# 88 unused columns at the end of the right-hand arena of a fused attention and two-layer feed-forward kernel

## Chip, core and metric

One core of one Trainium2 chip. The metric is the device time of one execution in microseconds (us); three runs of the kernel before were timed and their median is taken. One more execution was profiled, and all rows below come from it.

## What is computed

The program takes `q`, `k`, `v` of shape (4, 8, 576, 64), a feature matrix `omega` (128, 64) and five weight matrices, and runs three layers on 2304 tokens of width 512:

```python
def phi(x):
    proj = np.einsum('bhsd,md->bhsm', x, omega)
    h = proj - np.sum(x * x, axis=-1, keepdims=True) / 2.0
    return np.exp(h - np.max(h, axis=-1, keepdims=True)) / np.sqrt(m)
q_p, k_p = phi(q * scale), phi(k * scale)
kv = np.einsum('bhsm,bhsd->bhmd', k_p, v);  z = np.sum(k_p, axis=2)
x = (q_p @ kv) / (q_p . z + 1e-06)              # attention, (2304, 512)
h = x @ w_in                                    # (2304, 2048)
x = (h * sigmoid(h)) @ w_out                    # first feed-forward layer
g = x @ w_gate;  val = x @ w_val                # (2304, 1536) each
x = (g * sigmoid(g) * val) @ w_out2             # second feed-forward layer
```

All of it is in float32, and the weights come in as float64.

## The kernel before

**Stages.** Attention runs first (lines 678 to 966, up to about 122 us of the span). Then come four matmul phases: up 1 (`x @ w_in`, `up_phase`, line 1060, about 122 to 301 us), down 1 (`@ w_out`, `down_phase`, line 1308, to about 488 us), up 2 (`w_gate` and `w_val`, to about 756 us) and down 2 (`@ w_out2`, to the end).

**One product.** Each big matrix product is cut in 2 x 2 blocks and done with seven block products (`PROD`, `ORDER`) in place of eight. Every float32 operand is split in a high and a low part of type float32r, and a product is three matmuls: high weights by high data, high by low, low by high. So both up phases run one loop (line 1090) and both down phases another (line 1465), over matmuls of one kind: 128 x 128 weights and 384 moving columns.

```python
for l, r in ((wh, xh), (wh, xl), (wl, xh)):     # products, L1090
    nc.tensor.matmul(ps[b][:, :N], cut(l, j * P, P), cut(r, j * N, N), ...)
...
for c, (a, b) in enumerate(((wh, h), (wh, l), (wl, h))):   # down_phase, L1465
    nc.tensor.matmul(ps[BANKS[p] + e][:, :N], cut(a, e * P, P), b, ...)
```

**Where the operands lie.** TensorE reads them from three arenas in the on-chip memory, each cut in slots by hand (`cut`, line 101):

```python
ra = ra_p.tile([P, 21504], F32R, name="ra")       # right side
fa = ra_p.tile([P, 9984], F32, name="fa")         # right side, same pool
...
t = left.enter_context(tc.tile_pool(name=name, bufs=1)).tile([P, 10752], F32R, name=name)   # rb, rc
...
f_op = Free("operand", [cut(ra, X_AT + i * 768, 768) for i in range(14)])
```

`ra` and `fa` are taken from the right-hand end of the memory downward; `rb` and `rc` are taken from its left-hand start upward, when attention's own tiles are gone. `fa` holds the raw weights, the float32 intermediates and the results that go out; no matmul reads it. Slots, halves of slots and 128-column cuts all begin at multiples of 512 bytes from the start of their arena.

**Who reads what.** In the up phases the weights always lie in `ra` (six slots of 1792 columns, filled by `conv_job`, line 315), and the data lie in `ra`, `rb` or `rc`, one arena for each third of the tokens. In the down phases the weights lie in the slots of `f_op`, which are in all three arenas, and the data mostly in `ra` (`ZP`, `f_z`). A row of the trace names the arenas that a group of matmuls reads, data first: `ps<-rb,ra` has its data in `rb` and its weights in `ra`; `ps<-ra` has both in `ra`. While one matmul runs, the weights of the next one are loaded (engine PEld in the rows).

**Order of the work.** The program is written out by a planner in the kernel (`Op`, `Stream`, `flush`, lines 111 to 304). Its costs are constants and do not depend on addresses.

Of the kernel before, what the change touches and what calls it, by code (L numbers as in the profile page):

```python
# [9 lines left out]
F32 = mybir.dt.float32  # L10
# [32 lines left out]
def kernel(  # L43
# [15 lines left out]
    P = 128  # L59
# [34 lines left out]
    right = ctx.enter_context(ExitStack())  # L94
    ra_p = right.enter_context(tc.tile_pool(name="ra", bufs=1, side="right"))
    ra = ra_p.tile([P, 21504], F32R, name="ra")
    fa = ra_p.tile([P, 9984], F32, name="fa")
    pp = ctx.enter_context(tc.tile_pool(name="psum", bufs=1, space=PSUM))
    ps = [pp.tile([P, 512], F32, name=f"ps{i}") for i in range(8)]

# [1581 lines left out]
```

## Time and profile before

| what | value |
|---|---|
| runs, median (lowest to highest) | 896.62 us (895.88 to 896.86) |
| the profiled execution, its own time | 894.9 us |
| its span, first to last instruction | 893.1 us |
| TensorE matmul busy | 873.0 us, 98% of the span |
| TensorE weight load busy | 849.9 us, 95% |
| VectorE, ScalarE, GpSimd busy | 625.9, 548.4, 160.3 us |

The profiled execution lies 1.7 us below the median of the runs. The end of a matmul is modelled in the profile, and the next one begins before it; so the time that a matmul takes of TensorE is read from one start to the next, not from the duration in a row.

### The profile page before, as it was taken

The numbers are of one execution on the slowest core, as the hardware profiler recorded it, in microseconds if no ns is written. First come the engines' busy times: TensorE is split into PE (matmuls) and PEld (weight loads), VectorE is DVE, ScalarE is ACT, GpSimd is POOL, SyncE is SP. The second block draws the span as 40 slices with busy tenths as digits, with TensorE's granted clock in tenths as the row PEclk, the third lists the DMA queues.
The fourth block names the chain that finished last, engine by engine and source line by source line (L and its number), as shares of the span: only waits on it lengthen the run. The fifth ranks groups of instructions, "written<-read, shape, count | busy, mean of one in ns | idle before, by whom it ended". The sixth has DMA issues, their size and how long they took to land.

```text
span 893.1 us, 18094 instructions
## 1 busy us (share of the span) xinstructions
PE 873.0 (98%) x6882; PEld 849.9 (95%) x6882; DVE 625.9 (70%) x1016; ACT 548.4 (61%) x1166; POOL 160.3 (18%) x204
## 2 busy tenths in 40 slices
PE   8999999999999989999999999999999999999998
PEld 6888799999999989999998999999999999999998
DVE  4888876575733895785998898555555538977772
ACT  7989877766766754454466865454545356655452
POOL 0487920053330000000000044131212100000000
PEclk9999999999999999999999999999999999999999
DMA  7598676389999827427315567362625267563502
GB/s 262 187 310 262 241 243 196 138 274 298 293 329 387 290 94 225 122 76 241 109 59 184 164 206 239 115 196 95 195 95 171 77 234 240 174 237 108 176 1 72
DMA packets 105863, 170.08 MB, mean 190 GB/s; under 512 B 8752, under 2 KB 87984, under 8 KB 105776
## 3 DMA queue, kind: packets, MB, share of 16 engines
q1 hardware_dynamic: 105552, 168.69, 57.3%
q8 instruction: 54, 0.88, 0.4%
q10 hardware_dynamic: 224, 0.23, 0.1%
q14 instruction: 33, 0.27, 0.1%
HBM read 107.02 MB, written 61.87 MB: 189 GB/s over the span
## 4 chain that ended last, share of the span: by engine, by line
PE 84%; DMA 5%; DVE 5%; ACT 3%; issue 1%; SPq 1%; POOL 0%; ACTq 0%; DVEq 0%; POOLq 0%
PE ps L1090 44%; PE ps L1465 32%; PE ps L751 2%; PE ps L795 2%; PE ps L842 1%; PE ps L811 1%; DMA g_d<-fa 1%; DMA rawq<-in_q 1%; ACT kq L767 1%; DMA fa<-in_moe_w_in 1%; DVE ra L1328 1%; DMA fa<-in_moe_w_val 1%; PE ps L867 1%; DMA ra<-wu_val 1%; DMA wd_out<-fa 0%
## 5 line engine op out<-in xcount | busy, mean ns | idle before, releaser
L376 POOL TENSOR_TENSOR fa<-fa 128x256 f32<-128x256 f32 x124 | 101.2, 830 | 541.9 <-DVE fa L357 322.3
L1090 PE MATMUL ps<-rb,ra 128*128 128x384 f32 x840 | 156.9, 339 | 0.5 <-ACT ps L1107 0.5
L1090 PE MATMUL ps<-ra 128*128 128x384 f32 x840 | 155.8, 335 | 1.2 <-ACT ps L1107 1.2
L1090 PE MATMUL ps<-rc,ra 128*128 128x384 f32 x840 | 156.5, 339 | 0.0
L1090 PEld LDWEIGHTS ps<-rb,ra 128*128 128x128 f32 x840 | 148.3, 188 | 1.2 <-ACT ps L1107 1.2
L1090 PEld LDWEIGHTS ps<-ra 128*128 128x128 f32 x840 | 146.7, 188 | 2.0 <-ACT ps L1107 2.0
L1090 PEld LDWEIGHTS ps<-rc,ra 128*128 128x128 f32 x840 | 148.4, 188 | 0.1
L1164 DVE TENSOR_TENSOR fa<-fa,ps 128x384 f32<-128x384 f32 x120 | 66.2, 552 | 107.3 <-ACT ps L1107 81.5
L1107 ACT ACTIVATE ps<-ps 128x384 f32<-128x384 f32 x180 | 85.7, 476 | 83.6 <-PE ps L1090 77.0
L1324 ACT ACTIVATE ra<-fa 128x768 fp32r<-128x768 f32 x86 | 72.1, 844 | 67.8 <-PE ps L1465 54.5
L1328 DVE TENSOR_TENSOR ra<-fa,ra 128x768 fp32r<-128x768 f32 x81 | 77.5, 957 | 31.1 <-PE ps L1465 19.9
L1465 PE MATMUL ps<-ra,rb 128*128 128x384 f32 x516 | 98.1, 342 | 0.1
L1465 PEld LDWEIGHTS ps<-ra,rb 128*128 128x128 f32 x516 | 92.6, 190 | 0.9 <-DVE ra L1328 0.7
L1465 PE MATMUL ps<-ra,rc 128*128 128x384 f32 x482 | 90.5, 339 | 1.6 <-DVE ra L1328 1.6
L1465 PE MATMUL ps<-ra 128*128 128x384 f32 x486 | 87.3, 336 | 4.1 <-DVE ra L1328 3.7
L1465 PEld LDWEIGHTS ps<-ra 128*128 128x128 f32 x486 | 84.6, 188 | 5.3 <-DVE ra L1328 4.6
L1465 PEld LDWEIGHTS ps<-ra,rc 128*128 128x128 f32 x482 | 85.2, 188 | 2.8 <-DVE ra L1328 2.6
L767 ACT ACTIVATE kq<-ps,nb 128x128 f32<-128x128 f32 x288 | 79.3, 395 | 6.9 <-DVE nb L765 6.3
L1131 ACT ACTIVATE fa<-fa 128x384 f32<-128x384 f32 x84 | 43.8, 521 | 30.3 <-DVE fa L1164 30.1
L1348 DVE TENSOR_TENSOR fa<-ra,fa 128x768 f32<-128x768 f32 x63 | 60.1, 954 | 1.7 <-DMA ra<-g_d 1.0
L1131 ACT ACTIVATE fa<-ps 128x384 f32<-128x384 f32 x84 | 40.9, 487 | 23.2 <-PE ps L1090 22.9
L765 DVE TENSOR_REDUCE nb<-ps 128x4 f32<-128x512 f32 x72 | 48.4, 682 | 6.6 <-PE ps L751 3.9
(110 smaller groups left out, 1117.5 us busy)
## 6 DMA issues: line engine op xcount, KB each, us to landing
g_d<-fa SPq DMA_DIRECT2D x168, 192.0 KB, 3.1
fa<-g_d SPq DMA_DIRECT2D x42, 384.0 KB, 4.5
ra<-g_d SPq DMA_DIRECT2D x42, 384.0 KB, 3.8
fa<-in_moe_w_out SPq DMA_DIRECT2D x28, 512.0 KB, 5.5
fa<-in_moe_w_in SPq DMA_DIRECT2D x16, 512.0 KB, 5.7
wd_out<-fa SPq DMA_DIRECT2D x12, 512.0 KB, 3.3
fa<-in_moe_w_gate SPq DMA_DIRECT2D x12, 512.0 KB, 3.9
fa<-in_moe_w_val SPq DMA_DIRECT2D x12, 512.0 KB, 5.5
```

Of the source, the lines that this page charges most:

```text
L376: f(blk(f"S{n}"), blk(l), blk(r))
L751: nc.tensor.matmul(ps[2 * (d % 2) + h][t : t + D, o : o + M], raw[u, nm][r, c * P + t : c * P + t + D], om[r, :], start=True, stop=True, s ...
L765: nc.vector.reduce_max(nb, x, axis=AX.X, negate=True)
L767: nc.scalar.activation(e[:, g // 2, g % 2, h * M : (h + 1) * M], x[:, g, :], AF.Exp, bias=nb[:, g : g + 1])
L1090: nc.tensor.matmul(ps[b][:, :N], cut(l, j * P, P), cut(r, j * N, N), start=start and c == 0, stop=stop and c == 5, skip_group_check=True,)
L1107: nc.scalar.activation(out() if callable(out) else out, src, AF.Copy)
L1131: nc.scalar.activation(b["t"], src, AF.Silu)
L1164: nc.vector.tensor_add(t, t if in_place else p5[n], ps[bank_][:, :N])
L1324: nc.scalar.activation(ops[s, p, k][0], src(), AF.Copy)
L1328: nc.vector.tensor_sub(l, src(), h.bitcast(F32))
L1348: (nc.gpsimd if eng == "POOL" else nc.vector).tensor_sub(z(PLACE[to]), z(PLACE.get(l, l)), z(PLACE.get(r, r)))
L1465: nc.tensor.matmul(ps[BANKS[p] + e][:, :N], cut(a, e * P, P), b, start=p in FIRST and i == 0 and c == 0, stop=p in LAST and i == fp - 1 an ...
```

## The change

The tile `fa` becomes 88 columns (352 bytes in each partition) longer. No instruction reads or writes the new columns.

```diff
     ra_p = right.enter_context(tc.tile_pool(name="ra", bufs=1, side="right"))
     ra = ra_p.tile([P, 21504], F32R, name="ra")
-    fa = ra_p.tile([P, 9984], F32, name="fa")
+    fa = ra_p.tile([P, 9984 + 88], F32, name="fa")
```

Every tile on the right-hand side moves down by 352 bytes: `ra`, `fa`, and of attention's tiles those of the pool `v` (`v`, `st`, `nt`, `rc` of line 853, `ident`, `xt`, `xr1`). The rest stays. Each engine has the same instructions in the same order as before. The start of each arena in its partition, in bytes, as the two programs place them:

| arena | before | modulo 64 | modulo 512 | after | modulo 64 | modulo 512 |
|---|---|---|---|---|---|---|
| `ra` | 103392 | 32 | 480 | 103040 | 0 | 128 |
| `fa` | 189408 | 32 | 480 | 189056 | 0 | 128 |
| `rb` | 16512 | 0 | 128 | 16512 | 0 | 128 |
| `rc` | 59520 | 0 | 128 | 59520 | 0 | 128 |

## Rows read from the trace of the kernel before

**Rows 1.** The chain that ended last, shares of the span by line.

```profile
PE ps L1090 44%; PE ps L1465 32%; PE ps L751 2%; PE ps L795 2%; PE ps L842 1%; PE ps L811 1%; DMA g_d<-fa 1%; DMA rawq<-in_q 1%; ACT kq L767 1%; DMA fa<-in_moe_w_in 1%; DVE ra L1328 1%; DMA fa<-in_moe_w_val 1%; PE ps L867 1%; DMA ra<-wu_val 1%; DMA wd_out<-fa 0%
```

**Rows 2.** Busy time by stretch: bounds, length, engines' busy us (x instructions), granted clock, DMA.

```profile
128.70:236.30 107.60, 107.60 (x615) 107.60 (x614) 71.83 (x132) 76.98 (x170) 25.00 (x30) 1.00 0.73 238
258.48:298.30 39.82, 39.82 (x230) 39.82 (x231) 17.40 (x26) 27.88 (x56) 2.87 (x4) 1.00 0.98 357
329.40:468.50 139.10, 139.10 (x792) 138.57 (x791) 105.91 (x125) 70.43 (x103) 0.00 (x0) 1.00 0.44 135
492.62:516.10 23.48, 23.48 (x134) 23.48 (x134) 20.78 (x43) 18.89 (x42) 1.90 (x3) 1.00 0.50 159
535.24:755.92 220.68, 220.68 (x1255) 220.28 (x1256) 134.40 (x240) 114.71 (x235) 43.17 (x54) 1.00 0.50 163
773.01:889.00 115.99, 115.99 (x659) 115.69 (x659) 81.15 (x94) 55.35 (x81) 0.00 (x0) 1.00 0.37 120
```

**Rows 3.** The chain between those stretches, two of its longer pieces: start, us, what.

```profile
249.25 5.98 DMA fa<-in_moe_w_val
...
530.11 4.01 DMA fa<-in_moe_w_out
```

**Rows 4.** Up phases' matmuls by arena: count, busy us, mean ns, idle before.

```profile
L1090 PE MATMUL ps<-rb,ra 128*128 128x384 f32 x840 | 156.9, 339 | 0.5 <-ACT ps L1107 0.5
L1090 PE MATMUL ps<-rc,ra 128*128 128x384 f32 x840 | 156.5, 339 | 0.0
L1090 PE MATMUL ps<-ra 128*128 128x384 f32 x840 | 155.8, 335 | 1.2 <-ACT ps L1107 1.2
```

**Rows 5.** TensorE's timeline in down 1: start us, us, what, count.

```profile
367.11 19.93 PE L1465 MATMUL ps<-ra 128*128 128x384 f32 x114
386.88 20.30 PE L1465 MATMUL ps<-ra,rb 128*128 128x384 f32 x114
407.02 19.25 PE L1465 MATMUL ps<-ra,rc 128*128 128x384 f32 x108
426.10 19.92 PE L1465 MATMUL ps<-ra 128*128 128x384 f32 x114
445.87 10.30 PE L1465 MATMUL ps<-ra,rb 128*128 128x384 f32 x57
```

**Rows 6.** The same timeline in up 2.

```profile
616.57 3.34 PE L1090 MATMUL ps<-rc,ra 128*128 128x384 f32 x18
619.75 2.25 PE L1090 MATMUL ps<-ra 128*128 128x384 f32 x12
621.84 1.22 PE L1090 MATMUL ps<-rc,ra 128*128 128x384 f32 x6
622.90 4.33 PE L1090 MATMUL ps<-ra 128*128 128x384 f32 x24
627.06 1.22 PE L1090 MATMUL ps<-rb,ra 128*128 128x384 f32 x6
```

**Rows 7.** The same timeline in down 2.

```profile
874.12 4.32 PE L1465 MATMUL ps<-rb,rc 128*128 128x384 f32 x24
878.28 6.70 PE L1465 MATMUL ps<-ra,rc 128*128 128x384 f32 x37
```

**Rows 8.** The same timeline at the end of up 1.

```profile
280.44 20.96 PE L1090 MATMUL ps<-rc,ra 128*128 128x384 f32 x120
301.24 0.34 PE L1393 MATMUL ps<-ra 128*128 128x384 f32 x1
```

**Rows 9.** VectorE, one operation in two arenas, columns as in rows 4.

```profile
L1277 DVE TENSOR_TENSOR rb<-rb 128x768 fp32r<-128x768 f32 x10 | 9.6, 956 | 2.6 <-ACT rb L1273 1.1 <-DMA g_d<-fa 1.1 <-DMA rc<-wd_out 0.3
L1277 DVE TENSOR_TENSOR ra<-ra 128x768 fp32r<-128x768 f32 x9 | 8.5, 957 | 5.5 <-ACT ra L1273 5.4
```

**Rows 10.** Attention's transposes on TensorE, columns as in rows 4.

```profile
L811 PE MATMUL ps<-ident,kq 128*128 128x128 f32 x144 | 23.6, 287 | 0.0
...
L867 PE MATMUL ps<-ident,nt 128*128 128x128 f32 x72 | 11.8, 273 | 0.2 <-DVE nt L857 0.2
```

## The prediction

> **What bounds the kernel now.** I read the chain of waits first: the matmuls of lines 1090 and 1465, which are the four feed-forward phases, make up 76% of it [rows 1]. Then I cut the span where the chain leaves TensorE. In six long stretches TensorE is busy without a break, at the full granted clock of 2.4 GHz [rows 2]; there the only thing that sets the time is how fast one matmul follows another. Between the stretches the chain runs over loads, conversions and copies, transfers of 4 and 6 us among them [rows 3]; there a faster TensorE only waits longer.
>
> Next I looked for a difference between matmuls that do the same work. The up phases have 840 with data in each arena, all with weights in `ra`. Those with data in `ra` show 335 ns, the others 339 ns [rows 4]. As the ends are modelled, I went on to the timeline and divided the time from one group's start to the next group's start by its count; I call that the pitch.
>
> - In down 1, data are in `ra`. With weights in `ra`: (386.88 - 367.11) / 114 = 173.4 ns, and (445.87 - 426.10) / 114 = 173.4 ns. With weights in `rb`: (407.02 - 386.88) / 114 = 176.7 ns. With weights in `rc`: (426.10 - 407.02) / 108 = 176.7 ns [rows 5].
> - In up 2, with data in `rc` and weights in `ra`: (619.75 - 616.57) / 18 = 176.7 ns. Both in `ra`: (627.06 - 622.90) / 24 = 173.3 ns [rows 6].
>
> These groups alternate within one stage, with the same neighbours at work, so a stage's traffic does not explain the step of 3.3 ns. What goes with it is the place of the two operands: `ra` begins at 32 modulo 64, `rb` and `rc` at 0. Two different arenas at the same remainder are the test, and down 2 has it: data in `rb`, weights in `rc`, (878.28 - 874.12) / 24 = 173.3 ns [rows 7]. So two arenas cost nothing; unequal remainders do. Modulo 64 alone cannot be told from 128, 256 or 512 here, because all cuts are multiples of 512 bytes, but it need not be: after the change all three arenas are equal modulo 512.
>
> One stretch does not fit. At the end of up 1, 120 matmuls with data in `rc` and weights in `ra` run at (301.24 - 280.44) / 120 = 173.3 ns [rows 8]. Unequal remainders allow the slow pitch, then, but do not force it; TensorE and the loading of the next weights can also fall into a step in which nothing is lost.
>
> A rule speaks against the whole idea. The Trainium skill, "TensorE: Matmul & The Clock Gate", section "Step-by-step: what each phase is for", says that data and weights come through two independent read ports, so that loading the next weights takes no read bandwidth from the running matmul. By that rule the sum below would be zero. The rows differ from it by 3.3 ns a matmul, and the measurement decides.
>
> **The change, part by part.** No instruction is added, removed or moved, no queue is passed, no wait is new. What changes is addresses.
>
> *Matmuls of the feed-forward phases.* I take 173.5 ns as the pitch of every matmul after the change, between the 173.3 and 173.4 of the equal groups. What each stretch of rows 2 then gives back is its length less count times 173.5 ns:
>
> - 128.70 to 236.30: 107.60 - 615 x 0.1735 = 0.90 us
> - 258.48 to 298.30: 39.82 / 230 is 173.1 ns already, nothing
> - 329.40 to 468.50: 139.10 - 792 x 0.1735 = 1.69 us
> - 492.62 to 516.10: 23.48 - 134 x 0.1735 = 0.23 us
> - 535.24 to 755.92: 220.68 - 1255 x 0.1735 = 2.94 us
> - 773.01 to 889.00: 115.99 - 659 x 0.1735 = 1.65 us
>
> The sum is 7.41 us. Matmuls in the pieces between are faster too, but the chain is not on TensorE there, and I count nothing.
>
> Two things pull down. A short group behind a change of arena does not reach the best pitch: the 12 equal ones from 619.75 take (621.84 - 619.75) / 12 = 174.2 ns [rows 6], 0.7 above what I set. If that has a cause of its own and half of it stays on every matmul, the 3,455 in the five sums keep 1.2 us. And TensorE now arrives earlier at the pieces of rows 3, whose transfers and conversions partly follow their own queue. The DMA engines are 98% busy at 258 to 298 us [rows 2], so the 0.90 us won before may be spent as waiting behind that stretch. The bounds are therefore 7.4 us, and 7.4 - 1.2 - 0.9 = 5.3 us. I take 6.6 us, nearer the upper end, because long equal groups show no residue at all [rows 5], and TensorE waits nowhere in these stretches [rows 2], so what feeds it has some lead.
>
> *VectorE, ScalarE, GpSimd, DMA.* `ra` and `fa` move together, so their relation to each other stays. The same subtraction takes 956 ns in `rb` (0 modulo 64) and 957 ns in `ra` (32 modulo 64) [rows 9]: nothing. No transfer changes its size; I cost it at nothing, and were it to matter, it would be in the pieces between the stretches.
>
> *Attention.* `ident`, `nt`, `v` and `st` change their remainder, the weights in `kq` and `qp` do not. No row shows a price. The nearest is the 3.3 ns above: for the 144 + 72 transposes [rows 10] that is 0.7 us either way if all were on the path. With `kq` an unequal pair becomes equal, with `nt` it stays unequal, and the cuts of `v` and `st` are not multiples of 64 bytes, so they are mixed before and after. I take zero.
>
> The profiled execution took 894.9 us; less 6.6 that is 888.3. The runs' median is 1.7 us above it, 896.6, so for the median I forecast **890.0 us**, 0.7% faster. What can be told from no change is about 0.2%, or 1.8 us.
>
> **The rivals.**
>
> *Half is given back (chance 0.10).* The pitch falls, but each gain ends in a longer wait at the next piece of the chain that is not TensorE's. For it: VectorE is busy 106 of 139 us and 81 of 116 us in the down phases, so it has little room [rows 2]. Against it: 220 us run without one wait, so the work that feeds TensorE is not just in time. If half goes, 3.3 us remain: 893.3 us.
>
> *Nothing happens (0.07).* The remainders have no part in it: the step of 3.3 ns comes from something else that goes with `ra` beside another arena, such as the distance between them, and stays. For it are the 120 matmuls at 173.3 ns in unequal arenas [rows 8]. Against it is the pair `rb`, `rc`, also far apart, at the fast pitch [rows 7]. The time would be 896.6 us. The port rule of the Trainium skill, above, ends at this same time.
>
> *Slower (0.05).* Unequal pairs run in a slow step or, at the end of up 1, in a fast one [rows 8]. If equal arenas have a slow step too, the old kernel may have been thrown out of it at each change of arena, and an all-equal stream would stay in it from one wait to the next. The price is 3.3 ns on each matmul so caught: 11.4 us if all 3,455 are, against 7.4 us paid now, so 4.0 us more, 900.6 us. It decides from about two thirds of the matmuls (7.4 / 11.4) upward. Against it: two groups of 114 equal matmuls and one of 24 show not a trace of it [rows 5, 7].
>
> That the change doesn't do what it says is excluded by the placed addresses.
>
> **How the numbers follow.** The forecast has the remaining 0.78. Its own range, from the bounds of 5.3 and 7.4 us and 0.7 us for attention, is 888.5 to 892.0. Widened to the first rival it is 888.5 to 893.5, which leaves out the other two, 0.12. Faster by over 0.2% are the forecast and the first rival, 0.88; within it the second, 0.07; slower the third, 0.05.
>
> **What would show it.** In the profile after, all three rows of line 1090 should have one mean, about 335 ns, and groups of line 1465 with weights in `rb` or `rc` a pitch near 173.4 ns. The stretch that ran from 535 to 756 us should be about 2.9 us shorter, the one of 40 us at the end of up 1 as long as before. If the pitches fall but the span doesn't, the waits between the stretches have grown (first rival). If data in `rb` or `rc` with weights in `ra` still show 176.7 ns, the reason is wrong.

## The result, and the profile after

The kernel with the 88 columns takes **889.32 us** (median of four runs, 885.68 to 890.62), against 896.74 us for the kernel before, measured beside it. The ratio is 0.9913, with a 95% interval of 0.9889 to 0.9937: 0.9% faster, 0.7 us from the forecast and inside its range. The profiled execution took 888.82 us, its span is 887.0 us against 893.1.

The chain that ended last, shares of the span by line, as in [rows 1]:

```profile
PE ps L1090 37%; PE ps L1465 30%; PE ps L751 4%; PE ps L795 2%; DMA fa<-in_moe_w_out 2%; PE ps L842 2%; PE ps L811 2%; ACT kq L767 2%; DMA fa<-in_moe_w_in 1%; DVE fa L357 1%; DVE ra L423 1%; DVE ra L1328 1%; DMA ra<-g_d 1%; DVE fa L350 1%; POOL fa L376 1%
```

The two matmul lines are still two thirds of it. The six stretches of [rows 2] again, now bounded by the starts of the same first and last matmuls:

```profile
130.41:236.66 106.25, 106.25 (x614) 106.25 (x614) 71.89 (x132) 77.13 (x170) 24.73 (x30) 1.00 0.74 240
258.77:298.75 39.98, 39.98 (x231) 39.98 (x231) 17.55 (x26) 28.05 (x57) 2.87 (x4) 1.00 0.97 355
328.24:465.68 137.44, 137.44 (x791) 136.76 (x791) 106.22 (x125) 70.84 (x103) 0.00 (x0) 1.00 0.45 136
489.68:512.84 23.16, 23.16 (x133) 23.16 (x134) 20.67 (x43) 18.88 (x42) 1.80 (x2) 1.00 0.50 164
531.89:750.29 218.40, 218.25 (x1256) 217.61 (x1256) 133.97 (x240) 114.57 (x235) 43.34 (x54) 1.00 0.50 165
768.64:882.81 114.17, 114.17 (x658) 114.17 (x659) 80.55 (x94) 55.02 (x81) 0.00 (x0) 1.00 0.38 121
```

From the start of the same first matmul to the start of the same last one, the old trace took 107.71, 39.98, 139.11, 23.48, 220.70 and 115.68 us (up to 0.3 us from the lengths in [rows 2], whose bounds are not all starts of matmuls). The gains are 1.46, 0.00, 1.67, 0.32, 2.30 and 1.51 us, together **7.26 us**.

The up phases' matmuls by arena of the data, columns as in [rows 4]. The three means now differ by 1 ns:

```profile
L1090 PE MATMUL ps<-ra 128*128 128x384 f32 x840 | 155.6, 335 | 1.4 <-ACT ps L1107 1.4
L1090 PE MATMUL ps<-rb,ra 128*128 128x384 f32 x840 | 154.5, 334 | 0.6 <-ACT ps L1107 0.6
L1090 PE MATMUL ps<-rc,ra 128*128 128x384 f32 x840 | 154.2, 334 | 0.1
```

TensorE's timeline in down 1 (start us, us, what, count), the rows that answer to [rows 5]:

```profile
384.92 19.92 PE L1465 MATMUL ps<-ra,rb 128*128 128x384 f32 x114
404.68 18.88 PE L1465 MATMUL ps<-ra,rc 128*128 128x384 f32 x108
423.39 19.92 PE L1465 MATMUL ps<-ra 128*128 128x384 f32 x114
443.15 20.43 PE L1465 MATMUL ps<-ra,rb 128*128 128x384 f32 x114
```

With weights in `rb` the pitch is (404.68 - 384.92) / 114 = 173.3 ns, with weights in `rc` (423.39 - 404.68) / 108 = 173.2, with both in `ra` (443.15 - 423.39) / 114 = 173.3. The old 176.7 is gone. The same timeline in up 2, down 2 and at the end of up 1 [rows 6 to 8]:

```profile
554.60 3.28 PE L1090 MATMUL ps<-rb,ra 128*128 128x384 f32 x18
557.72 2.24 PE L1090 MATMUL ps<-rc,ra 128*128 128x384 f32 x12
...
619.08 4.32 PE L1090 MATMUL ps<-ra 128*128 128x384 f32 x24
623.24 1.20 PE L1090 MATMUL ps<-rb,ra 128*128 128x384 f32 x6
...
872.59 6.57 PE L1465 MATMUL ps<-ra,rc 128*128 128x384 f32 x37
879.00 0.33 PE L1465 MATMUL ps<-rb,rc 128*128 128x384 f32 x1
...
280.72 20.96 PE L1090 MATMUL ps<-rc,ra 128*128 128x384 f32 x120
301.52 0.33 PE L1393 MATMUL ps<-ra 128*128 128x384 f32 x1
```

In this order: (557.72 - 554.60) / 18 = 173.3 ns, (623.24 - 619.08) / 24 = 173.3, (879.00 - 872.59) / 37 = 173.2, (301.52 - 280.72) / 120 = 173.3. All are at the fast pitch, the last as before.

**What the span kept.** Of the 7.26 us the span shows 6.1; the pieces ahead of, between and behind the stretches took 1.16 us more. Three of them matter.

- The first stretch begins at 130.41 instead of 128.72 us, 1.69 later. In this execution TensorE was granted half clock (1.2 GHz) in the attention stage, after its first matmuls. That does not explain the later begin: a second profile of the changed kernel has full clock there and begins its first stretch at 130.34 us. Columns as in [rows 2], first the execution above, then the second one:

```profile
10.10:13.52 3.42, 3.42 (x49) 2.97 (x49) 1.29 (x2) 1.89 (x8) 0.00 (x0) 0.50 1.04 363
10.10:13.52 3.42, 3.42 (x82) 2.78 (x72) 2.13 (x4) 3.10 (x12) 0.00 (x0) 1.00 1.05 357
```

- Between the second stretch and the third the pieces took 29.49 instead of 31.03 us, 1.54 less. There the old execution had its half clock, behind a wait of 2.3 us. Its row, columns as in [rows 2]:

```profile
325.88:329.29 3.41, 3.41 (x12) 3.41 (x11) 2.37 (x4) 0.69 (x1) 0.00 (x0) 0.50 0.00 0
```

- Early in down 2 a wait grew. TensorE's timeline there, first of the old kernel, then of the changed one (idle before, and who released it, in brackets):

```profile
770.46 2.42 PE L1465 MATMUL ps<-rb 128*128 128x384 f32 x13
773.01 0.45 PE L1465 MATMUL ps<-ra,rb 128*128 128x384 f32 x1
```

```profile
765.01 2.52 PE L1465 MATMUL ps<-rb 128*128 128x384 f32 x13
768.64 0.44 PE L1465 MATMUL ps<-ra,rb 128*128 128x384 f32 x1 [1.10 <-DVE ra L1328]
```

The 13 matmuls and the wait took 773.01 - 770.46 = 2.55 us before and 3.63 now: TensorE arrives earlier and waits for VectorE's subtraction of line 1328. The whole piece between the last two stretches took 17.07 us before and 18.35 now.

### The profile page after: what moved, and what is told of

Read it like the earlier page. It is cut to its first block, busy times and chain, and to the rows that moved or that the text cites. A ratio compares the mean times of both kernels' runs of the same rounds, so it can differ in the third digit from the quotient of the medians.

```text
span 887.0 us, 18094 instructions
## 1 busy us (share of the span) xinstructions
PE 866.2 (98%) x6882; PEld 842.3 (95%) x6882; DVE 623.9 (70%) x1016; ACT 548.6 (62%) x1166; POOL 160.2 (18%) x204
## 4 chain that ended last, share of the span: by engine, by line
PE 77%; DVE 8%; DMA 6%; ACT 4%; issue 3%; POOL 1%; SPq 1%; DVEq 0%; ACTq 0%; POOLq 0%
PE ps L1090 37%; PE ps L1465 30%; PE ps L751 4%; PE ps L795 2%; DMA fa<-in_moe_w_out 2%; PE ps L842 2%; PE ps L811 2%; ACT kq L767 2%; DMA fa<-in_moe_w_in 1%; DVE fa L357 1%; DVE ra L423 1%; DVE ra L1328 1%; DMA ra<-g_d 1%; DVE fa L350 1%; POOL fa L376 1%
## 5 line engine op out<-in xcount | busy, mean ns | idle before, releaser
L1090 PE MATMUL ps<-rb,ra 128*128 128x384 f32 x840 | 154.5, 334 | 0.6 <-ACT ps L1107 0.6
L1090 PE MATMUL ps<-rc,ra 128*128 128x384 f32 x840 | 154.2, 334 | 0.1
L1090 PEld LDWEIGHTS ps<-rb,ra 128*128 128x128 f32 x840 | 146.3, 188 | 1.3 <-ACT ps L1107 1.3
L1090 PEld LDWEIGHTS ps<-rc,ra 128*128 128x128 f32 x840 | 146.3, 188 | 0.4 <-ACT ps L1107 0.4
L1465 PE MATMUL ps<-ra,rb 128*128 128x384 f32 x516 | 95.4, 335 | 1.1 <-DVE ra L1328 1.1
L1465 PEld LDWEIGHTS ps<-ra,rb 128*128 128x128 f32 x516 | 89.9, 188 | 2.0 <-DVE ra L1328 1.9
```

## The experiments

The question left open was which property of the addresses sets the pitch. Each kernel below moves arenas and nothing else. I name it by one number d: the address of the data less the address of the weights that are loaded meanwhile, modulo 512 bytes. All cuts are multiples of 512 bytes, so d is the difference of two arena starts. (Whether a period shorter than 512 bytes would describe it as well is not tested.) With both operands in `ra` it is 0, except where said. In the kernel before, d is 128 - 480 = 160 in the up phases (data in `rb` or `rc`, weights in `ra`) and 352 in the down phases (the other way round). In the changed one it is 0 everywhere.

The table gives for each kernel the summed length of the six stretches in its profiled execution, between the same matmuls throughout, and the time. The stretches leave out attention and most waits, so they tell kernels apart that the times do not. Each ratio is to runs of the kernel before made beside that kernel; their medians were 896.1 to 896.8 us.

| kernel | d, up / down | six stretches, us | median us (runs) | ratio to before, 95% interval |
|---|---|---|---|---|
| before | 160 / 352 | 646.7 | 896.74 (4) | |
| before, second profile | 160 / 352 | 647.0 | 895.08 (1) | |
| the change | 0 / 0 | 639.4 | 889.32 (4) | 0.9913 [0.9889, 0.9937] |
| the change, second profile | 0 / 0 | 639.6 | 890.16 (1) | |
| 8 columns | 192 / 320 | 640.0 | 890.03 (4) | 0.9937 [0.9913, 0.9961] |
| 24 columns | 256 / 256 | 639.6 | 885.87 (1) | |
| 48 columns | 352 / 160 | 646.3 | 894.65 (7) | 0.9972 [0.9953, 0.9990] |
| 80 columns | 480 / 32 | 643.0 | 891.22 (6) | 0.9943 [0.9923, 0.9962] |
| `ra` against itself | 0; in `ra` 32 / 480 | 640.4 | 889.89 (4) | 0.9936 [0.9916, 0.9956] |
| all at 32 | 32 / 480 | 642.3 | 893.00 (5) | 0.9947 [0.9924, 0.9971] |
| left moved by 8 columns | 192 / 320 | 640.4 | 889.87 (4) | 0.9925 [0.9902, 0.9948] |
| left moved by 88 columns | 0 / 0 | 640.1 | 891.05 (4) | 0.9931 [0.9909, 0.9952] |
| offsets of 16 bytes | 16, 48 / 464 to 496 | 644.2 | 897.80 (1) | |

**8 columns.** All arenas become equal modulo 64, but not modulo 512.

```diff
-    fa = ra_p.tile([P, 9984], F32, name="fa")
+    fa = ra_p.tile([P, 9984 + 8], F32, name="fa")
```

> 8 columns in place of 88: all arenas begin at 0 modulo 64, but ra at 448 and rb, rc at 128 modulo 512, so ra and the others still differ modulo 128. Theory (only the remainder modulo 64 counts): pitch 173.4 ns in every group, about 889 us, ratio to before 0.991. Rival (the relation counts at 128 bytes or more): mixed groups stay at 176.7 ns, 896.7 us, ratio 1.000.

The stretches are within 0.6 us of the change, and the intervals of the two ratios overlap. Equality modulo 64 was enough here, but for one part of up 2, in which mixed groups (d = 192) took neither of the two pitches. TensorE's timeline at its start and behind its end:

```profile
551.37 2.26 PE L1090 MATMUL ps<-rb,ra 128*128 128x384 f32 x12
...
565.00 1.20 PE L1090 MATMUL ps<-ra 128*128 128x384 f32 x6
```

Between the two starts lie 78 matmuls: (565.00 - 551.37) / 78 = 174.7 ns.

**80 columns.** `ra` stays at 32 modulo 64 and `rb`, `rc` at 0, but the distance is another.

```diff
-    fa = ra_p.tile([P, 9984], F32, name="fa")
+    fa = ra_p.tile([P, 9984 + 80], F32, name="fa")
```

> 80 columns: ra moves by 320 bytes, about as far as in the change, but stays at 32 modulo 64. Theory: the mixed groups of line 1090 keep a mean of 339 ns and the pitch 176.7 ns, 896.7 us, ratio 1.000. Rival (any move of that size, or the new distance to the other arenas, does it): 335 ns, 889 us, ratio 0.991. Also to be seen: whether the end of up 1 again runs at 173.3 ns in spite of unequal remainders.

Two stretches within up 1 and down 1, columns as in [rows 2]:

```profile
135.00:230.00 95.00, 95.00 (x549) 95.00 (x548) 60.83 (x115) 68.03 (x150) 21.11 (x25) 1.00 0.71 235
335.00:460.00 125.00, 125.00 (x714) 124.78 (x713) 93.03 (x107) 61.55 (x88) 0.00 (x0) 1.00 0.47 141
```

In up 1 (d = 480) 549 matmuls pass in 95 us, where the kernel before has 542 and the change 550: nearly all fast. In down 1 (d = 32) 714 pass in 125 us, where the kernel before has 713 and the change 721: slow. Half of the gain is there although the remainders modulo 64 are as unequal as before. The time, 891.2 us, lies between the 896.7 of my test and the 889 of its rival. My test, "unequal remainders do cost", falls. What counts is the difference itself, and its sign.

**48 columns.** The two old differences change places.

```diff
-    fa = ra_p.tile([P, 9984], F32, name="fa")
+    fa = ra_p.tile([P, 9984 + 48], F32, name="fa")
```

> 48 columns: ra begins at 288 modulo 512. Data less weights are 352 in the up phases and 160 in the down phases where before they are 160 and 352: the two differences of the old kernel with their roles exchanged. Theory A (unequal modulo 64 costs): 896.7 us, 176.7 ns in all mixed groups. Theory B with the difference setting which step is taken: the same, 896.7 us, since both differences ran slow before. Rival (something particular to the old placement): 889 to 892 us.

The same two stretches, and TensorE's timeline at the end of up 1:

```profile
135.00:230.00 95.00, 94.84 (x540) 94.52 (x539) 59.36 (x111) 67.19 (x148) 20.43 (x24) 1.00 0.70 231
335.00:460.00 125.00, 125.00 (x721) 124.79 (x720) 94.22 (x107) 61.99 (x87) 0.00 (x0) 1.00 0.46 140
```

```profile
281.17 2.28 PE L1090 MATMUL ps<-rb,ra 128*128 128x384 f32 x12
283.29 19.95 PE L1090 MATMUL ps<-rc,ra 128*128 128x384 f32 x112
```

d = 352 is slow in up 1 too, (283.29 - 281.17) / 12 = 176.7 ns, and at its end, where 160 had run fast [rows 8]. d = 160, slow in the old up 1, runs fast through this down 1 (721 matmuls) and slow in down 2, whose last stretch takes 115.4 us, nearly the old 115.7. So 352 was slow wherever I saw it, and 160 has both paces.

**`ra` against itself.** `ra` begins at 128 modulo 512 like `rb` and `rc`, so mixed pairs have d = 0; but its own data slots lie 32 bytes further, so pairs within `ra` have 32.

```diff
-    ra = ra_p.tile([P, 21504], F32R, name="ra")
-    fa = ra_p.tile([P, 9984], F32, name="fa")
+    ra = ra_p.tile([P, 21504 + 8], F32R, name="ra")
+    fa = ra_p.tile([P, 9984 + 80], F32, name="fa")
...
-    W_AT, T_AT, X_AT = 0, 7168, 10752
+    W_AT, T_AT, X_AT = 0, 7168, 10752 + 8
```

> ra, rb, rc begin at 0 modulo 64, but the operand slots inside ra are 8 columns further, at 32. In the up phases data in ra now differ from the weights, and data in rb and rc agree with them. Theory: roles are turned round; in line 1090 the group with data in ra has the longer mean, about 339 ns and a pitch of 176.7 ns, those with rb and rc 335 ns and 173.4 ns. 1,460 of 4,288 pairs of a matmul and the next one's weights are unequal in place of 2,753, so 1,460 x 3.0 ns = 4.4 us over the changed kernel: about 893.5 us, ratio 0.9965. Rival (which arenas are paired, not their remainders): as before, ra the fastest, 896.7 us; or all fast, 889 us.

TensorE's timeline at the start of up 1:

```profile
128.65 16.14 PE L1090 MATMUL ps<-ra 128*128 128x384 f32 x90
144.62 1.23 PE L1090 MATMUL ps<-rb,ra 128*128 128x384 f32 x6
145.69 2.24 PE L1090 MATMUL ps<-ra 128*128 128x384 f32 x12
147.77 2.42 PE L1090 MATMUL ps<-rb,ra 128*128 128x384 f32 x13
```

The 90 matmuls within one arena, never slow before, take (144.62 - 128.65) / 90 = 177.4 ns (176.6 without one hold-up of 0.08 us at their start, which the other kernels have too). So the loss does not need two arenas, only two addresses. Behind the first six mixed matmuls the same kind of pair runs at (147.77 - 145.69) / 12 = 173.3 ns, and stays near it in most of up 1 and up 2. One difference, two paces; here no hold-up but six matmuls with another difference lay between. So most of the loss that my test forecast for this kernel (893.5 us) did not come.

**All at 32.** The kernel above, with `rb` and `rc` moved 32 bytes too: now every up-phase matmul has d = 32.

```diff
-        t = left.enter_context(tc.tile_pool(name=name, bufs=1)).tile([P, 10752], F32R, name=name)
+        t = left.enter_context(tc.tile_pool(name=name, bufs=1)).tile([P, 10752 + 8 * (name == "rb")], F32R, name=name)
...
-            f_op.give(cut(t, i * 768, 768))
+            f_op.give(cut(t, 8 * (name == "rb") + i * 768, 768))
```

> All data of the up phases are 32 bytes (modulo 512) above the weights, and nearly all of the down phases 32 below: 3,857 of 4,288 pairs unequal modulo 64, but the difference hardly changes within a phase. Theory A (unequal modulo 64 costs 3.0 ns each): 3,857 x 3.0 = 11.6 us over the changed kernel, 901 us, ratio 1.005, pitch 176.7 ns nearly everywhere. Theory B (there is a slow and a fast step, a fixed difference may run in either, and the step is set anew at a wait or a change of difference): each phase mostly in one step, between 889 and 901 us. Theory C (only changes of the difference cost): 173.4 ns, 889 us, ratio 0.992.

Up 1 is slow from end to end (its first two stretches take 108.3 and 40.6 us, where the change has 106.3 and 40.0). Up 2, with the same difference, is fast (218.1 us against 218.4), but for 11 us. TensorE's timeline at their end:

```profile
547.82 4.41 PE L1090 MATMUL ps<-rb,ra 128*128 128x384 f32 x24
552.06 1.30 PE L1090 MATMUL ps<-rc,ra 128*128 128x384 f32 x6
553.20 2.24 PE L1090 MATMUL ps<-rb,ra 128*128 128x384 f32 x12
555.28 1.20 PE L1090 MATMUL ps<-rc,ra 128*128 128x384 f32 x6
```

(552.06 - 547.82) / 24 = 176.7 ns, then 553.20 - 552.06 = 1.14 us for six, 0.10 more than six fast ones take, and from there (555.28 - 553.20) / 12 = 173.3 ns. The difference stayed the same, and the change from `rb` to `rc` alters no pace elsewhere in this phase; what came in between was a short hold-up of TensorE. So matmuls and weight loads can run in at least two steps with one difference, and behind such a hold-up the stream can be in another one than before it.

**The left side moved, by 8 and by 88 columns.** `ra` and `fa` stay; `rb` and `rc` move up by 32 or by 352 bytes.

```diff
-        t = left.enter_context(tc.tile_pool(name=name, bufs=1)).tile([P, 10752], F32R, name=name)
+        t = left.enter_context(tc.tile_pool(name=name, bufs=1)).tile([P, 10752 + 8 * (name == "rb")], F32R, name=name)
...
-            f_op.give(cut(t, i * 768, 768))
+            f_op.give(cut(t, 8 * (name == "rb") + i * 768, 768))
```

With 88 in place of both 8s it is the second kernel.

> ra and fa stay where they were, at 32 modulo 64; rb and rc move by 32 bytes to 32 as well. Theory (only equality counts): 173.4 ns everywhere, 889 us, ratio 0.991. Rival (a begin at 0 modulo 64 is what counts): as before or slower, 896.7 us or more, all groups at 176.7 ns.

> ra and fa stay at 480 modulo 512, and rb and rc move there: all equal modulo 512 as in the change, but at another place. Theory B' (with difference 0 only the fast step occurs, wherever the arenas lie): 173.3 ns in every group and every stretch, 889 us, ratio 0.991. Rival (the place of ra at a multiple of 128 bytes is what the change gained by): slow stretches of 176.7 ns remain, 892 us or more.

Both come out where the change does, in time and in stretches. What is won belongs to the relation of the arenas and not to the place of `ra`, `fa` or attention's tiles. With 8 columns (d = 192) one slow part is left, behind a wait in up 2:

```profile
550.18 2.28 PE L1090 MATMUL ps<-rb,ra 128*128 128x384 f32 x12
552.30 1.22 PE L1090 MATMUL ps<-rc,ra 128*128 128x384 f32 x6
...
565.03 2.24 PE L1090 MATMUL ps<-rc,ra 128*128 128x384 f32 x12
567.11 1.21 PE L1090 MATMUL ps<-ra 128*128 128x384 f32 x6
```

(552.30 - 550.18) / 12 = 176.7 ns, and 15 us later (567.11 - 565.03) / 12 = 173.3. So equal remainders modulo 64 do not shut the slow step out. And the difference alone does not fix the pace of a step: with `ra` 8 columns lower, the same groups at the same difference took 174.7 ns, above.

**Both kernels profiled again, and 24 columns.** The first two have no edit. The third makes the arenas equal modulo 256, but not 512.

```diff
-    fa = ra_p.tile([P, 9984], F32, name="fa")
+    fa = ra_p.tile([P, 9984 + 24], F32, name="fa")
```

> The kernel before once more, for a second profile. If the difference and the waits set the step: the same stretches slow (mixed groups 176.7 ns in up 1 from 144 us on, in down 1, up 2 and down 2) and the same fast (the end of up 1 after the wait at 258 us, and the 12 us after the wait at 553 us at 173.3 ns). If it is chance: other stretches.

> The changed kernel once more, for a second profile. Theory B': again 173.3 ns in all long groups, after each of its waits too, since difference 0 has shown no slow stretch. Rival (it was in the fast step by chance): one or more stretches at 176.7 ns.

> 24 columns: the arenas are equal modulo 64, 128 and 256 and differ by 256 modulo 512. If a difference that is a multiple of 64 runs fast unless a wait throws it out, as 192 and 320 did: 173.3 ns with at most one short slow stretch, about 889 to 891 us. If 256 is like 160 and 352: 176.7 ns, 896 us.

The kernel before shows the same slow and fast parts again. Among them is a fast part in up 2 behind a hold-up, where the same pair ran slow until then; TensorE's timeline in its second profile:

```profile
545.88 2.28 PE L1090 MATMUL ps<-rb,ra 128*128 128x384 f32 x12
548.00 1.21 PE L1090 MATMUL ps<-ra 128*128 128x384 f32 x6
...
554.58 2.24 PE L1090 MATMUL ps<-rb,ra 128*128 128x384 f32 x12
556.66 1.20 PE L1090 MATMUL ps<-rc,ra 128*128 128x384 f32 x6
```

(548.00 - 545.88) / 12 = 176.7 ns and (556.66 - 554.58) / 12 = 173.3. The changed kernel and the one with 24 columns have no slow part anywhere, but for a few matmuls behind a hold-up: 639.4 to 639.6 us in the stretches. The time of the latter, 885.87 us, is one run, and one of the change took 885.68; it is no evidence of a further gain.

**Offsets of 16 bytes.** The change, with `rb` at 16 and `rc` at 48 bytes from `ra`, modulo 512.

```diff
-    fa = ra_p.tile([P, 9984], F32, name="fa")
+    fa = ra_p.tile([P, 9984 + 88], F32, name="fa")
...
-        t = left.enter_context(tc.tile_pool(name=name, bufs=1)).tile([P, 10752], F32R, name=name)
+        t = left.enter_context(tc.tile_pool(name=name, bufs=1)).tile([P, 10752 + 8], F32R, name=name)
...
-            f_op.give(cut(t, i * 768, 768))
+            f_op.give(cut(t, 4 + i * 768, 768))
```

> The change with its 88 columns, but the slots in rb lie 16 bytes and those in rc 48 bytes (modulo 64) off those in ra. Theory A (any inequality modulo 64): mixed groups at 176.7 ns, 896 us. If a step of 16 bytes does not count and only 32 does: 173.4 ns, 889 us. Theory B: in between, each stretch at either 173.3 or 176.7 ns.

TensorE's timeline in up 1:

```profile
152.09 19.11 PE L1090 MATMUL ps<-rb,ra 128*128 128x384 f32 x108
171.05 1.21 PE L1090 MATMUL ps<-rc,ra 128*128 128x384 f32 x6
...
174.20 19.06 PE L1090 MATMUL ps<-rc,ra 128*128 128x384 f32 x108
193.10 1.21 PE L1090 MATMUL ps<-ra 128*128 128x384 f32 x6
```

With d = 16 the pitch is (171.05 - 152.09) / 108 = 175.6 ns, with d = 48 (193.10 - 174.20) / 108 = 175.0, over 19 us each without a hold-up. I had expected 173.3 or 176.7; it is neither. So there are more than two paces. The stretches take 644.2 us, so two thirds of the old loss are back (4.8 of 7.3). The time of the one run is not to be read so: its first stretch begins at 133.5 us, 3.1 later than in the change, after a part at half clock in attention.

## Why the prediction was right, point by point

**The sum.** Forecast for the six stretches were 0.90, 0, 1.69, 0.23, 2.94 and 1.65 us, together 7.41; the same matmuls gave 1.46, 0.00, 1.67, 0.32, 2.30 and 1.51, together 7.26. The first was set too low, since its row counts 615 matmuls where 613 lie from the first start to the last one. Up 2 fell short by 0.6: 1,255 matmuls at 173.5 ns are 217.7 us, and the stretch took 218.4, with 0.15 us of idle time in its row and hold-ups of a few tenths where TensorE now comes early. The second profile gives 7.0 us (646.66 - 639.63).

**The two subtractions.** No residue of short groups stayed: over all feed-forward matmuls the changed kernel is 0.16 us above 173.4 ns each (start to start, hold-ups over 200 ns left out), the kernel before 8.44. The 174.2 ns that I read from a short group [rows 6] are in part the rounding of two starts (0.01 us over 12 matmuls is 0.8 ns; unrounded it is 173.8). The rest goes with the change of the difference, which the changed kernel no longer has. With 80 columns it is larger: six matmuls with both operands in `ra`, behind a mixed group, take 1.07 us there (610.28 to 611.35) in place of 1.04. The 0.90 us at the full DMA engines was not given back as a longer wait: the piece between the first two stretches took 22.05 us before and 22.11 now. It was taken up, though, by the later end of attention, so the two can't be parted in this profile. The kernel with 24 columns parts them: it came to that piece at 235.59 us, the kernel before at 236.43, and the piece took no longer (21.49 us).

**The first rival** came true in one place. What down 2's last stretch won, 1.51 us, is nearly eaten by the piece ahead of it, which grew from 17.07 to 18.35 us (17.30 to 18.04 in the second profiles). It is no fixed price, though: with 24 columns, at the same pace, that piece took 17.21 us. Of the other pieces none grew by 0.1 us, so most of the gain stayed, as the argument from the lead of the feeding engines had it. The reading behind that argument, "220 us run without one wait", was too strong: by the starts, TensorE was already held up in the old up 2 for 0.2 us at 542 us and for 0.06 at 553; the modelled ends hide it.

**The second rival** did not come: the 176.7 ns of the mixed groups went when the difference became 0. Its doubt about the remainders was right, though. What counts is the distance between the two operands, taken modulo 512, and not equality modulo 64. The port rule of the Trainium skill ("TensorE: Matmul & The Clock Gate", "Step-by-step: what each phase is for") gave the same time as that rival, no gain. The trace does not agree with it as a rule for time: in the slow step a matmul takes 3.3 ns longer, 2%, though it reads the same bytes.

**The third rival, slower,** asked whether equal arenas have a slow step too. Four profiles have d = 0 throughout or d = 256: none shows it, behind any of their waits. But its premise held. There is more than one step; the kernel before was in the fast one at the end of up 1, and the kernel with every pair at 32 stays in the slow one through a whole phase.

**Attention** was taken as zero. Its transposes kept their durations, whose ends are modelled (287 ns for line 811 and 273 for line 867 in the second profile of the change, the same as in [rows 10]). Its end varies even where its tiles lie the same. Where they lie as before, the first stretch begins at 128.7 and 128.3 us (the kernel before), 129.7 and 134.0 (left side moved by 8 and by 88 columns); where they lie as in the change, at 130.4 and 130.3 (the change), 133.5 (offsets of 16 bytes) and 128.9 (`ra` against itself). The executions with 134.0 and 133.5 have a part at half clock in attention, but so has the one with 130.4; the cause of the spread stays open. A loss of about a microsecond in attention by the change is not shown, and these few profiles do not exclude it.

**The step that failed** is the test: "two arenas cost nothing; unequal remainders do". What the runs showed is that the pace goes with the difference modulo 512, and that some differences allow more than one. Only slow, 176.7 ns: 352. Both slow and fast: 32, 160, 192, the last at 174.7 ns too. In between, at 175.0 to 175.6 ns in up 1: 16 and 48. Only fast in long runs: 0 and 256 in all phases, 320 in the down phases, and 480, whose first matmuls behind a change of the difference are slower. The time came out right because the change makes the difference 0, and arenas that are equal modulo 512 are equal modulo 64 too; by the same test 80 columns would have been forecast as no change, and they gained 5 us (896.08 to 891.22).

**What stays open.** Why the loads and the matmuls have several steps, which of them a hold-up leads to, and why 352 has no fast one, these runs don't tell. They show where, not how.

## What to carry to other kernels

Read TensorE's pace from start to start, by the arenas of its two operands: two values within one stage, under the same traffic, point to addresses. Let the tiles that feed data and weights begin at equal addresses modulo 512 bytes: 0 and 256 are the differences that were seen here in all phases without a slow part, and the padding cost only memory. And check where TensorE arrives early afterwards: a gain may be spent waiting for the next operation that feeds it.

## What the runs showed that was not expected

One fixed difference of addresses can run 2% slow for over 160 us and fast for 200 us in one execution (d = 32, up 1 and up 2), and the pace changed there at a hold-up of 0.1 us.

Short parts at half clock come and go between executions of one kernel: behind the wait of 2.3 us in down 1 in both profiles of before and in the second of the change, but not in the first of the change, which has one at its start. In down 1 it is worth some 1.5 us: over all 13 profiles, the piece between the second and third stretch takes 30.65 to 31.03 us with it and 29.46 to 29.50 without. The end of attention moves by 2 us between most of the profiles, and by more in two. Both are more than some of the differences tested here; so I compared stretches between the same matmuls, and not times alone.
